# Seven products for w_out from tile 38 on, not 36; ten of batch 6's sixteen inverse blocks in one train with the last batch's, six ahead of it

## The chip, the cores and the metric

The kernel runs on one core of one Trainium2 chip. The metric is the device time of one execution in microseconds (us), the median of several runs.

## The reference

Two parts follow each other: a spectral layer (FFT along the sequence, a complex mix of 256 channels, soft shrinkage, inverse FFT) and a feed-forward part with a squared ReLU. All data are float32; 8 sequences (batches) of 3008 positions with 256 channels, 2048 hidden channels.

```
X = np.fft.rfft(x, axis=1)
Yr = Xr @ w_r - Xi @ w_i + b_r
Yi = Xr @ w_i + Xi @ w_r + b_i
Yr = np.sign(Yr) * np.maximum(np.abs(Yr) - lam, 0.0)
Yi = np.sign(Yi) * np.maximum(np.abs(Yi) - lam, 0.0)
y = np.fft.irfft(Y, n=x.shape[1], axis=1)
...
h = x @ w_in
r = np.maximum(h, 0.0)
g = r * r
return (g @ w_out).astype(np.float32)
```

## The kernel before

**Tiles and steps.** The feed-forward part runs over 48 tiles, six for each batch; a tile t holds about 500 positions, in two halves of 250 or 252. Batch 6 is tiles 36 to 41, batch 7 tiles 42 to 47. A tile is worked in 8 steps n, each on two of the 16 blocks of hidden channels. A step's first part (`first`, four products, 12 matmuls on TensorE) and second part (`second`, three products, 9 matmuls) multiply by w_in with seven products for a 2 by 2 block scheme; every product is three matmuls, since each number is split into a high and a low part. Their results are in four banks named psh; VectorE combines them (mp, mu, mv, mc), ScalarE squares and makes the high part mg, GpSimd the low part (`mg<-mc,mg`, two halves). Two steps later `out` multiplies by w_out into the two banks named pso: 6 matmuls for each of two halves, 12 of 500 columns in all. The main loop runs over m, half steps, so a step is two units of m and a tile 16. `then` fixes the order of these instructions on each engine.

**Seven products for w_out.** For tiles in `FREE`, in steps 1, 3 and 5 of the eight (`SEVEN`), `out_seven` takes seven products there as well: 21 matmuls of 250 columns instead of 12 of 500. It needs sums of the weights (`out_sums`, GpSimd), sums of g (`forms`), and two banks named psf that hold part of the results from step 1 to the end of the tile (`part`, `tile_sums`).

**The other work.** Between those steps stands the spectral layer of the later batches, as a list of jobs with a due time in units of m: forward blocks (`fwd_tasks`), pairs of frequency groups (`pair_tasks`: `fwd`, `mix`, `shrink`, `back`, lines 289, 310 and 343) and inverse blocks (`Back`, lines 553, 556 and 557). An inverse block gives 188 positions: for each of two channel halves three matmuls into one psf bank, a copy on ScalarE and an addition on VectorE (dy). All these share the two psf banks with the seven products. For each of the batches 6 and 7 all 16 blocks are computed ahead of their tiles: `load` or `load_two` (two blocks in one load, tiles th, tl, ts) fetches du from DRAM, `mm` computes, `keep` stores dy to DRAM (y), and `raw_load` fetches a whole tile's share back (yr) when its tile comes near. From yr the token sums are made: in `back_tasks` for ordinary tiles (`Tokens.sums`, `Tokens.split`, GpSimd and ScalarE), and by `Tokens.free` during the tile before where that tile is in `FREE`. `Tokens.free` keeps its sums in the tile ts, whose one buffer is also that of `load_two`.

**Where batches 6 and 7 stand.** `kept_tasks(B - 2, ...)` puts batch 6 into four groups of four blocks, a group every 16 units from 486.55 on, blocks 2.2 units apart; u, u2 and dy of such a block are all in the three buffers of xt. The pairs of batch 7 run from 489 to 547 at 5.25 units. `late` opens the tiles th, tl, ts and wsh, wsl, and the 16 blocks of batch 7 follow as a train from 554.85 on, 1.4 units apart. Tile 36 begins at 576.

**Order.** What `then` doesn't fix is placed by a scheduler that works with estimated times; the order on each engine is fixed before the program runs. DMAs that load are chained on SyncE's queue (`load_next`), which also issues the stores.

Of the kernel before, what the change touches and what calls it, by code (L numbers as in the profile page):

```python
# [24 lines left out]
B, S, D, FF = 8, 3008, 256, 2048  # L25
# [5 lines left out]
HALF = (252, 252, 250, 250, 250, 250)  # L31
HM = max(HALF)
NF = FF // 128
# [23 lines left out]
B11, B21, B22, T1, T3, T2, T4 = range(7)  # L57
ENDS = B - 2
TURN0, TURNS, PACE = 92, J, 6
FREE = range(ENDS * len(HALF), B * len(HALF) - 1)  # L60
SEVEN = (1, 3, 5)


# [1 line left out]
def fnet_moe(ctx: ExitStack, tc, x, w_r, w_i, b2, w_in, w_out, bm, cm, dx, am2, a32, c32, d32, out):  # L65
# [34 lines left out]
    def T(name, shape, dt, tag=None):  # L100
        tag = tag or name
        return pools.get(tag, phase["pool"]).tile(shape, dt, name=name, tag=tag, bufs=phase["bufs"].get(tag, 2))

    def bank(shape, name="psf"):
        return phase["psum"].tile(shape, F32, name=name, tag=name, bufs=phase["bufs"].get(name, 1))
# [281 lines left out]
    class Fwd32(Fwd):  # L387
# [8 lines left out]
        def mm(self):  # L396
            n = self.n
            self.ps = []
            for t in range(2):
                u = T("x2", [M1, 2, D], F32, tag="small")  # L400
                eng = pool if t and self.r == 1 else dve
                cut = eng.tensor_tensor(
                    out=u[:, :n], in0=self.xt[:M1, :n, 0], in1=self.xt[:M1, :n, 1], op=(ALU.add, ALU.subtract)[t]
                )
                if eng is pool:
                    self.far = cut
                else:
                    self.cut = cut
                ps = bank([128, 2, D])
                nc.tensor.matmul(ps[:M1, :n], am32[:, t], u[:, :n], start=True, stop=True)  # L410
                self.ps.append(ps)
# [85 lines left out]
    W2 = 4 * N2  # L497
    raw, yts, back_last = {}, {}, {}

    class Back:  # L500
# [40 lines left out]
        def mm(self):  # L541
            if self.b == 0:
                return self.mm32()
            if self.b == ENDS or self.b > ENDS and self.q % 5 % 2 == 0:
                y = T("dy", [128, 512], F32, tag="xt")[:, :2 * W2].rearrange("p (c w) -> p c w", c=2)
            else:
                y = T("dy", [128, 2, W2], F32)
            self.y = y
            for c in range(2):
                cs = slice(c * 128, c * 128 + 128)  # L550
                ps = bank([128, 2, 256])[:, :, :W2]
                pv = ps.rearrange("c j (p t) -> c j p t", p=2)
                mm = nc.tensor.matmul(pv[:, :, 0], self.u[:, 0, cs], dx_sb[:, 0], start=True, stop=False)  # L553

                with tc.issue_after(mm.ins):
                    nc.tensor.matmul(pv[:, :, 1], self.u[:, 1, cs], dx_sb[:, 0], start=False, stop=False)  # L556
                nc.tensor.matmul(ps[:, 0], self.u2[:, cs], dx_sb[:, 1], start=False, stop=True)  # L557
                self.done = copy(act, y[:, c], ps[:, 1])
                if self.b >= ENDS:
                    self.cut = dve.tensor_add(out=y[:, c], in0=ps[:, 0], in1=y[:, c])  # L560
                    continue
                for n, (t, lo, hi, at) in enumerate(self.spans):
                    if n == c == 0 and t not in raw:
                        raw[t] = T("yr", [128, 2, 2 * HM], F32)
                    o = y[:, c, lo:hi] if n else raw[t][:, c, at:at + hi - lo]
                    self.cut = dve.tensor_add(out=o, in0=ps[:, 0, lo:hi], in1=y[:, c, lo:hi])
# [141 lines left out]
    class Step:  # L708
        def __init__(self, t, n):
            self.t, self.n, self.h = t, n, tiles[t][2]  # L710
            self.end = t == len(tiles) - 1 and n == NF // 2 - 1
            self.seven = t in FREE and n in SEVEN

        def product(self, ps, a, b, terms=range(3)):
            yh, yl = yts[self.t]
# [69 lines left out]

        def out_seven(self, j):
            t, h, n = self.t, self.h, self.n
            i = SEVEN.index(n)
            if i == j == 0:
                part[t] = [bank([128, 512])[:, :2 * h].rearrange("p (j h) -> p j h", j=2) for _ in range(2)]  # L790
            low, high = [a[:, :2 * h].rearrange("p (j h) -> p j h", j=2) for a in acc[t]]
            p16, p57 = part[t]
            f = 2 * n
            plain = [[w[:, f + k, d * 128:(d + 1) * 128] for w in wout] for d, k in ((0, 0), (0, 1), (1, 1))]
            sums = [[w[:, i, k] for w in ws] for k in range(4)]
            g, tf = self.g, (self.th, self.tl)
            if j == 0:
                todo = ((p16[:, 0], plain[0], g, 0), (low[:, 0], plain[1], g, 2), (low[:, 1], sums[3], g, 3))
            else:
                todo = (  # L800
                    (p57[:, 0], sums[0], tf, 0), (p57[:, 1], sums[2], tf, 1),
                    (p16[:, 1], sums[1], tf, 2), (high[:, 0], plain[2], tf, 3),
                )
            for q, (x, y) in enumerate(((0, 0), (1, 0), (0, 1))):
                for at, (ps, a, b, k) in enumerate(todo):
                    then(
                        pe, pe.matmul, ps, a[x], b[y][:, k],
                        start=i == q == at == 0, stop=i == len(SEVEN) - 1 and q == 2 and j == 1 and at in (1, 2),
                    )

        def finish(self, pc, pd):
# [17 lines left out]
        def out(self, j):  # L829
# [14 lines left out]
            if f == NF - 1:  # L844
                b, c0, _ = tiles[t]
                if t in FREE:
                    o = last_sums.pop(t)
                else:
                    o = T("mo", [128, 4 * HM], F32, tag="ms")[:, :4 * h].rearrange("p (d h) -> p d h", d=2)
                for d in range(2):  # L850
                    if t in FREE:
                        then(dve, dve.tensor_add, out=o[:, d], in0=acc[t][d][:, :2 * h], in1=o[:, d])
# [35 lines left out]
    def back_tasks(t, start):  # L888
        b, c0, h = tiles[t]
        new = range(-(-c0 // W2), -(-(c0 + 2 * h) // W2))  # L890
        if b >= ENDS:
            new = ()
        jobs = []
        for j, q in enumerate(new):
            k, at = Back(b, q), start + 2.2 * j
            back_last[t] = k
            ahead = 1.6 if j == 0 and t > 1 and t % len(HALF) == 1 else 0.55 if j else 0.0
            jobs += [(at - ahead, k.load), (at + 1.6, (lambda k=k: behind(k.mm)) if t == 1 else k.mm)]
            if len(k.spans) > 1:
                jobs += [(start + 14.6, k.put)]  # L900
        if t > FREE[0]:
            return [(start, lambda: raw_load(t))]
        if t == FREE[0]:
            jobs += [(start, lambda: raw_load(t))]
        k = Tokens(t)
        if t == 0:
            return jobs + [(start + 7.1, k.begin)]
        for j in range(2):
            jobs += [(start + 7.1 + j, lambda j=j: k.sums(j))]
        for j in range(4):  # L910
            jobs += [(start + 9.1 + 1.2 * j, lambda j=j: k.split(j))]
        return jobs

    def raw_load(t):
        b, c0, h = tiles[t]
        raw[t] = T("yr", [128, 2, 2 * HM], F32)
        load_next(raw[t][:, :, :2 * h], ys[b][:, :, c0:c0 + 2 * h])

    def kept_tasks(b, start, step, wait):
        ks = [Back(b, q) for q in range(S // W2)]  # L920
        jobs = []
        for q, k in enumerate(ks):
            if b < B - 1:
                at = start + NF * (q // 4) + step * (q % 4)
                jobs += [(at, k.load)]
            else:
                at = start + step * q
                if q % 2 == 0:
                    jobs += [(at, lambda k=k, o=ks[q + 1]: k.load_two(o))]
            jobs += [(at + wait, k.mm), (at + wait + 1.0, k.keep)]  # L930
        return jobs

    def late():
# [82 lines left out]
    for r in range(-1, len(units) + 3):  # L1016
# [5 lines left out]
        k = r - 2  # L1022
# [12 lines left out]
        n, odd = divmod(k, 2)  # L1035
# [5 lines left out]
        if k >= 1 and odd and early:  # L1041
            q = early.pop(0)
# [35 lines left out]
    first = sorted(back_tasks(0, 0), key=lambda j: j[0])  # L1078
    kind = {"load": 0, "mm": 1}
    first = [[job for _, job in first if kind.get(job.__name__, 2) == k] for k in range(3)]  # L1080
# [25 lines left out]
    jobs = []  # L1106
# [7 lines left out]
    for b in range(2, B):  # L1114
        start = TURN0 + (b - 2) * TURNS * PACE
# [1 line left out]
        if b + 1 < B:  # L1117
            jobs += fwd_tasks(b + 1, start + 4)
    for t in range(1, len(tiles)):
        jobs += back_tasks(t, NF * (t - 1) + (-1.5 if t == FREE[0] else 0.5))  # L1120
    over = TURN0 + (B - 3) * TURNS * PACE
    jobs += kept_tasks(B - 2, NF * 30 + 6.55, 2.2, 2.15)
    done = over + PACE + 1.0 + 11 * 5.25 + 7.5
    jobs += [(done + 0.5, late)] + kept_tasks(B - 1, done + 0.6, 1.4, 2.4)
    jobs += [(done + 3.0 + 6.0 * j, lambda n=n: out_sums(n)) for j, n in enumerate(SEVEN)]
    jobs.sort(key=lambda j: j[0])
    for m in range(2 * len(steps) + 4):
        n, k = divmod(m, 2)
        if k and 0 <= n - 2 < len(steps):
            steps[n - 2].out(1)  # L1130
        if n < len(steps):
            t, i = divmod(n, NF // 2)
            ahead = k and t in FREE and i in (0, 2, 4, 6)
# [117 lines left out]
```

## Time and profile before

| | us |
|---|---|
| median of 3 runs (lowest to highest) | 2592.17 (2591.49 to 2594.46) |
| the profiled execution | 2589.44 |
| its span, first to last instruction | 2587.5 |
| TensorE matmul busy in the span | 2565.2 |
| VectorE / GpSimd / ScalarE busy | 1907.2 / 1761.2 / 1417.7 |

TensorE is called busy for 99% of the span, but a matmul's busy time runs on while the next has begun, so a busy TensorE may be working below its pace. The chain of work that ended last is TensorE for 97%. The granted clock is full but for two short stretches; the page's 40 slices show one of them.

### The profile page before, as it was taken

The numbers are of one execution on the slowest core, as the hardware profiler recorded it, in microseconds if no ns is written. First come the engines' busy times: TensorE is split into PE (matmuls) and PEld (weight loads), VectorE is DVE, ScalarE is ACT, GpSimd is POOL, SyncE is SP. The second block draws the span as 40 slices with busy tenths as digits, with TensorE's granted clock in tenths as the row PEclk, the third lists the DMA queues.
The fourth block names the chain that finished last, engine by engine and source line by source line (L and its number), as shares of the span: only waits on it lengthen the run. The fifth ranks groups of instructions, "written<-read, shape, count | busy, mean of one in ns | idle before, by whom it ended". The sixth has DMA issues, their size and how long they took to land.

```text
span 2587.5 us, 48058 instructions
## 1 busy us (share of the span) xinstructions
PE 2565.2 (99%) x17507; PEld 2373.7 (92%) x17507; DVE 1907.2 (74%) x3797; ACT 1417.7 (55%) x2175; POOL 1761.2 (68%) x1684
## 2 busy tenths in 40 slices
PE   9999999999999999999999999999999999999999
PEld 7899999999999999999999999999898989999998
DVE  7876766777777777777777777776676668888886
ACT  5655555555555555555555555555555545555554
POOL 1167666777676776677767676675555858888885
PEclk9999999999999999999999999999999989999999
DMA  9632332333333333433333333434334321000000
GB/s 312 197 94 86 113 101 76 108 110 106 102 107 113 103 109 102 119 106 102 104 111 113 109 99 106 118 97 119 118 112 124 119 85 33 23 27 25 25 25 17
DMA packets 192001, 257.03 MB, mean 99 GB/s; under 512 B 18376, under 2 KB 138176, under 8 KB 191768
## 3 DMA queue, kind: packets, MB, share of 16 engines
q1 hardware_dynamic: 178353, 228.71, 28.7%
q0 software_dynamic: 13280, 25.16, 4.1%
q8 instruction: 140, 2.29, 0.4%
q14 instruction: 93, 0.76, 0.1%
q10 hardware_dynamic: 135, 0.12, 0.0%
HBM read 150.36 MB, written 103.55 MB: 98 GB/s over the span
## 4 chain that ended last, share of the span: by engine, by line
PE 97%; DVE 2%; DMA 1%; ACT 0%; issue 0%; POOL 0%; SPq 0%; DVEq 0%; POOLq 0%; ACTq 0%
PE pso L592 38%; PE psh L592 36%; PE psf L310 7%; PE psf L289 3%; PE psf L343 2%; PE psf L251 2%; PE psf L592 2%; PE psf L475 1%; PE psf L557 1%; PE psf L556 1%; PE psf L553 1%; PE psf L373 1%; PE psf L530 1%; PE psf L410 0%; PE psf L485 0%; PE psf L461 0%
## 5 line engine op out<-in xcount | busy, mean ns | idle before, releaser
L113 POOL TENSOR_TENSOR mg<-mc,mg 128x500 fp32r<-128x500 f32 (+1 forms) x766 | 995.3, 1320 | 402.8 <-ACT mg L109 304.4
L592 PE MATMUL pso<-mg,wout 128*128 128x500 f32 (+2 forms) x4311 | 1086.1, 389 | 2.7 <-POOL mg L113 2.7
L592 PE MATMUL psh<-yt,win 128*128 128x250 f32 (+1 forms) x8064 | 1072.9, 280 | 0.8 <-DVE mc L592 0.3
L592 PEld LDWEIGHTS psh<-yt,win 128*128 128x128 f32 x8064 | 1019.0, 189 | 27.5 <-DVE yt L113 0.6
L592 PEld LDWEIGHTS pso<-mg,wout 128*128 128x128 f32 x4311 | 773.3, 189 | 125.7 <-POOL mg L113 3.0
L592 ACT ACTIVATE mc<-mc 128x1000 f32<-128x1000 f32 (+1 forms) x384 | 400.4, 1043 | 458.7 <-DVE mc L592 457.7
L592 DVE CUSTOM_DVE_ANT_0 mc<-psh,mv 128x250 f32<-128x250 f32 (+3 forms) x769 | 418.6, 546 | 286.3 <-PE psh L592 244.1
L109 ACT CAST mg<-mc 128x1000 fp32r<-128x1000 f32 (+1 forms) x385 | 396.8, 1031 | 14.5 <-POOL mg L113 0.4
L592 DVE TENSOR_TENSOR mv<-psh,mu 128x500 f32<-128x500 f32 (+1 forms) x384 | 260.9, 679 | 46.8 <-PE psh L592 12.4
L310 PE MATMUL psf<-wx,kxh 128*128 128x256 f32 x1008 | 211.4, 283 | 3.0 <-ACT kxh L109 1.3
L110 DVE COPY mp<-psh 128x250 f32<-128x250 f32 (+1 forms) x384 | 160.2, 417 | 53.1 <-PE psh L592 29.4
L331 DVE TENSOR_TENSOR kv<-psf,ke 64x256 f32<-64x256 f32 x336 | 141.8, 422 | 51.1 <-PE psf L310 35.6
L310 PEld LDWEIGHTS psf<-wx,kxh 128*128 128x128 f32 x1008 | 168.2, 190 | 6.1 <-ACT kxh L109 1.5
L592 DVE TENSOR_TENSOR mu<-psh,mp 128x250 f32<-128x250 f32 (+1 forms) x384 | 160.9, 419 | 12.4
L222 POOL TENSOR_TENSOR xs<-xt 120x256 f32<-120x256 f32 x156 | 120.0, 789 | 61.9 <-DMA xt<-x_in 21.7
L592 DVE CUSTOM_DVE_ANT_0 mc<-psh,mp 128x250 f32<-128x250 f32 (+1 forms) x384 | 156.8, 408 | 6.4 <-PE psh L592 6.3
L113 POOL TENSOR_TENSOR ksl<-kv,ksh 128x512 fp32r<-128x512 f32 x84 | 109.5, 1304 | 70.7 <-ACT ksh L109 66.4
L109 ACT COPY dy<-psf 128x188 f32<-128x188 f32 (+2 forms) x229 | 71.3, 314 | 152.7 <-PE psf L557 150.5
L310 PE MATMUL psf<-wx,kxl 128*128 128x256 f32 x504 | 142.2, 282 | 0.3 <-DVE kxl L113 0.3
L113 POOL TENSOR_TENSOR yt<-yr,yt 128x250 fp32r<-128x250 f32 (+1 forms) x94 | 88.3, 939 | 36.9 <-ACT yt L109 36.4
L333 ACT ACTIVATE kc<-kv,low 128x512 f32<-128x512 f32 x84 | 60.8, 724 | 84.5 <-DVE kv L331 84.3
L322 DVE TENSOR_TENSOR ke<-psf,bias 128x512 f32<-128x512 f32 x84 | 57.8, 688 | 59.2 <-PE psf L310 59.0
(164 smaller groups left out, 3180.5 us busy)
## 6 DMA issues: line engine op xcount, KB each, us to landing
ka<-s SPq DMA_DIRECT2D x96, 256.0 KB, 3.0
du<-s SPq DMA_DIRECT2D x96, 256.0 KB, 2.9
kcm<-cm_in POOLq DMA_DIRECT2D x84, 256.0 KB, 3.8
s<-kuh SPq DMA_DIRECT2D x84, 256.0 KB, 3.5
s<-kul SPq DMA_DIRECT2D x84, 256.0 KB, 3.7
s<-xe SPq DMA_DIRECT2D x82, 240.0 KB, 2.4
xt<-x_in SPq DMA_DIRECT2D x81, 240.0 KB, 3.2
out<-mo SPq DMA_DIRECT2D x64, 250.0 KB, 2.2
```

What stands on the lines that cost most here:

```text
L109: return act.copy(out=out, in_=in_)
L110: return eng.tensor_copy(out=out, in_=in_)
L113: return eng.tensor_tensor(out=out, in0=a, in1=b, op=ALU.subtract)
L222: return eng.tensor_tensor(out=out[:, :n], in0=self.xt[:, :n, 0], in1=self.xt[:, :n, 1], op=(ALU.add, ALU.subtract)[t])
L251: nc.tensor.matmul(ps[:, t], am_sb[0][:, j, t], v[:, t], start=n == 0, stop=n == 2)
L289: nc.tensor.matmul(pv[:, :, c, g, :], self.a[:, g, c * 128:(c + 1) * 128], bg, start=True, stop=True)
L310: self.last = nc.tensor.matmul(ps, l, wx[j][:, k, c, :], start=n == 0, stop=n == 5)
L322: dve.tensor_add(out=self.e, in0=self.pe, in1=bias)
L331: dve.tensor_add(out=v[64 * r:64 * r + 64, g], in0=ps[gs], in1=self.e[gs, r])
L333: act.activation(r, v, AF.Relu, bias=low)
L343: nc.tensor.matmul(ps[:, g], self.cm[:, g, j * 128:(j + 1) * 128], r[:, g], start=n == 0, stop=n == 2)
L592: last_of[eng] = op(*args, **kwargs)
```

## The change

- `FREE` begins at tile 38: tiles 36 and 37 take the ordinary 12 matmuls in all eight steps and get their token sums from `back_tasks`; so does tile 38, while 39 to 46 go on as before.
- `SPARE = 6`: of batch 6's 16 blocks the first six stand alone, from 488 on, 10.5 units apart, with 3.4 units from load to matmul (it was 2.15). Their dy is in xt.
- The other ten are put at the head of batch 7's train and loaded two at a time with `load_two`: 26 blocks from 554.85 on, 1.4 units apart, where there were 16. Their dy buffers alternate between dy and xt as batch 7's do.
- The loads of yr for tiles 36 to 38 come 2.5 units later than their jobs' start; that of 36 came 2 units before the usual start.
- In `Step` and `out_seven` the list of steps becomes a member (`sevens`); for the tiles that use it, it is the same list.

```diff
-FREE = range(ENDS * len(HALF), B * len(HALF) - 1)
+FREE = range(ENDS * len(HALF) + 2, B * len(HALF) - 1)
+SPARE = 6
...
-            if self.b == ENDS or self.b > ENDS and self.q % 5 % 2 == 0:
+            if self.b >= ENDS and (self.b == ENDS and self.q < SPARE or self.q % 5 % 2 == 0):
...
-        if t == FREE[0]:
-            jobs += [(start, lambda: raw_load(t))]
+        if b >= ENDS:
+            jobs += [(start + 2.5, lambda: raw_load(t))]
...
-    def kept_tasks(b, start, step, wait):
-        ks = [Back(b, q) for q in range(S // W2)]
+    def kept_tasks(ahead, start, step):
+        first, *ks = [[Back(b, q) for q in range(S // W2)] for b in range(ENDS, B)]
+        ks = first[SPARE:] + ks[0]
         jobs = []
+        for q, k in enumerate(first[:SPARE]):
+            at = ahead + 10.5 * q
+            jobs += [(at, k.load), (at + 3.4, k.mm), (at + 4.4, k.keep)]
         for q, k in enumerate(ks):
-            if b < B - 1:
-                at = start + NF * (q // 4) + step * (q % 4)
-                jobs += [(at, k.load)]
-            else:
-                at = start + step * q
-                if q % 2 == 0:
-                    jobs += [(at, lambda k=k, o=ks[q + 1]: k.load_two(o))]
-            jobs += [(at + wait, k.mm), (at + wait + 1.0, k.keep)]
+            at = start + step * q
+            if q % 2 == 0:
+                jobs += [(at, lambda k=k, o=ks[q + 1]: k.load_two(o))]
+            jobs += [(at + 2.4, k.mm), (at + 3.4, k.keep)]
...
-        jobs += back_tasks(t, NF * (t - 1) + (-1.5 if t == FREE[0] else 0.5))
+        jobs += back_tasks(t, NF * (t - 1) + 0.5)
     over = TURN0 + (B - 3) * TURNS * PACE
-    jobs += kept_tasks(B - 2, NF * 30 + 6.55, 2.2, 2.15)
     done = over + PACE + 1.0 + 11 * 5.25 + 7.5
-    jobs += [(done + 0.5, late)] + kept_tasks(B - 1, done + 0.6, 1.4, 2.4)
+    jobs += [(done + 0.5, late)] + kept_tasks(over + 6.0, done + 0.6, 1.4)
```

The order on the engines differs from m = 486 to about m = 614 and is the same elsewhere. Lines of the changed kernel are one higher from line 61 on, two from 714 on. Names: psf is one of the two shared banks, psh and pso those of the products with w_in and w_out, kb,ka a pair's first products, wx its mix, dx_sb,du an inverse block.

TensorE at m = 544, in tile 34 before the change: a pair's first products, two half blocks and the next mix, with no product of the tile between them.

```order
L289 MATMUL psf<-kb,ka 128x2x64 x4
L553 MATMUL psf<-dx_sb,du 128x2x94
L556 MATMUL psf<-dx_sb,du 128x2x94
L557 MATMUL psf<-dx_sb,du 128x188
L553 MATMUL psf<-dx_sb,du 128x2x94
L556 MATMUL psf<-dx_sb,du 128x2x94
L557 MATMUL psf<-dx_sb,du 128x188
L310 MATMUL psf<-wx_81,kxh 128x256
```

The same pair's first products in the changed kernel (m = 546):

```order
L593 MATMUL psh_25184<-yt_24900,win_84 128x250
L344 MATMUL psf<-ksl,kcm 128x256
L344 MATMUL psf<-ksh,kcm 128x256 x2
L344 MATMUL psf<-ksl,kcm 128x256
L593 MATMUL psh_25184<-yt_24901,win_83 128x250
L593 MATMUL psh_25268<-yt_24900,win_83 128x250
L593 MATMUL psh_25268<-yt_24900,win_84 128x250
L290 MATMUL psf<-kb,ka 128x2x64 x4
```

In the piece before, 15 groups on psf follow each other from m = 543.9 to 544.5 with three short runs of psh matmuls between them; in the changed order no more than five do anywhere from 486 on, and most stand alone between products of the tile.

TensorE at m = 581, where tile 36's first step is multiplied by w_out, before the change (nine half blocks in a row follow from the third row from the end on):

```order
L592 MATMUL pso_26854<-mg_26739,wout_86 128x504
L553 MATMUL psf<-dx_sb,du 128x2x94
L556 MATMUL psf<-dx_sb,du 128x2x94
L557 MATMUL psf<-dx_sb,du 128x188
L592 MATMUL pso_26855<-mg_26739,wout_85 128x504
L592 MATMUL pso_26855<-mg_26739,wout_86 128x504
L553 MATMUL psf<-dx_sb,du 128x2x94
L556 MATMUL psf<-dx_sb,du 128x2x94
L557 MATMUL psf<-dx_sb,du 128x188
```

The same place in the changed kernel:

```order
L593 MATMUL pso_26665<-mg_26543,wout_85 128x504
L554 MATMUL psf<-dx_sb,du 128x2x94
L557 MATMUL psf<-dx_sb,du 128x2x94
L558 MATMUL psf<-dx_sb,du 128x188
L593 MATMUL pso_26666<-mg_26543,wout_85 128x504
L593 MATMUL psh_26643<-yt_26233,win_83 128x252
```

The train's last half block stands at m = 601 now (it was 581), one at a time, and the first matmul of the seven products at m = 615 (it was 583). On GpSimd, the first use of the tile ts by `Tokens.free` at the start of tile 36, before the change:

```order
L113 TENSOR_TENSOR mg_26580<-mc,mg_26579 128x500 x2
L113 TENSOR_TENSOR mg_26652<-mc,mg_26651 128x500 x2
L113 TENSOR_TENSOR ts<-yr 128x252 x2
L113 TENSOR_TENSOR mg_26740<-mc,mg_26739 128x504 x2
L592 TENSOR_TENSOR ts<-yr,ts 128x252
```

And in the changed kernel, at the start of tile 38:

```order
L114 TENSOR_TENSOR mg_27511<-mc,mg_27510 128x504 x2
L114 TENSOR_TENSOR mg_27566<-mc,mg_27565 128x504 x2
L114 TENSOR_TENSOR ts<-yr 128x250 x2
L114 TENSOR_TENSOR mg_27626<-mc,mg_27625 128x500 x2
L593 TENSOR_TENSOR ts<-yr,ts 128x250
```

It moved from the end of the train to some 14 units behind it. SyncE's queue around the load of yr for tile 36, before:

```order
L120 DMA du<-s_7_75 128x1024
L120 DMA du<-s_7_75 64x2x256 x2
L120 DMA yr<-y_76 128x2x504
L858 DMA out<-mo 128x500 x2
L580 DMA y_77<-dy 256x1x188
```

and in the changed kernel:

```order
L581 DMA y_76<-dy 256x1x188
L121 DMA du<-s_6_74 128x1024
L121 DMA du<-s_6_74 64x2x256 x2
L581 DMA y_76<-dy 256x1x188
L121 DMA yr<-y_76 128x2x504
L581 DMA y_76<-dy 256x1x188
```

The load of yr stood behind the train's second pair of blocks, and stands behind the third now, and behind two stores.

## Rows read from the trace of the kernel before

**Rows 1.** Stretches: busy PE, PEld, DVE, ACT, POOL; clock, DMA share, GB/s.

```profile
1500.00:1800.00 300.00, 300.00 (x2075) 278.93 (x2074) 217.26 (x439) 167.33 (x262) 208.03 (x202) 1.00 0.37 106
1800.00:2115.00 315.00, 301.22 (x1999) 276.08 (x1999) 200.96 (x442) 158.21 (x264) 188.16 (x186) 0.96 0.39 118
```

**Rows 2.** Chain, full clock: start us, us, engine, line, matmuls.

```profile
1808.57 0.09 PE psf L553
1808.66 0.11 PE psf L556
1808.77 0.11 PE psf L557
...
1823.71 1.41 PE psf L310 x12
...
1849.03 0.71 PE psf L343 x6
...
1945.98 0.89 PE psf L289 x8
```

**Rows 3.** The chain: two steps' products with w_out, one after the other.

```profile
1949.09 2.74 PE pso L592 x12
...
1974.05 2.07 PE pso L592 x8
```

**Rows 4.** Matmuls, 1948.92 to 1974.05 us: count, busy, mean ns, idle, releasers.

```profile
L310 PE MATMUL psf<-wx,kxh 128*128 128x256 f32 x24 | 6.6, 346 | 1.7 <-DVE dy L566 0.6 <-DVE kul L113 0.6 <-DVE dy L560 0.5
...
L310 PE MATMUL psf<-wx,kxl 128*128 128x256 f32 x12 | 4.0, 333 | 0.0
...
L553 PE MATMUL psf<-dx_sb,du 128*128 128x188 f32 x7 | 2.6, 365 | 1.6 <-PE psf L289 0.6 <-DVE ke L322 0.4 <-DMA du<-s 0.3
...
L343 PE MATMUL psf<-ksh,kcm 128*128 128x256 f32 x8 | 2.0, 350 | 0.0
L343 PE MATMUL psf<-ksl,kcm 128*128 128x256 f32 x4 | 1.4, 350 | 0.0
```

**Rows 5.** The chain around tile 36's first product with w_out.

```profile
2079.79 2.49 PE pso L592 x11
...
2103.32 2.91 PE psh L592 x21
```

**Rows 6.** Matmuls by form, 2079.63 to 2103.11 us, as rows 4.

```profile
L592 PE MATMUL pso<-mg,wout 128*128 128x504 f32 x12 | 5.0, 561 | 2.7 <-POOL mg L113 2.7
L553 PE MATMUL psf<-dx_sb,du 128*128 128x188 f32 x12 | 4.4, 365 | 2.9 <-DVE dy L560 1.8 <-DMA du<-s 0.8
```

**Rows 7.** Waits, 1800 to 2115 us: in total, times, longest.

```profile
POOL ts L113 <- PE psf L557: 19.4, 1, 19.4
```

**Rows 8.** Shorter stretches, columns as rows 1.

```profile
1963.63:1974.05 10.42, 9.40 (x40) 8.49 (x41) 3.71 (x9) 2.39 (x6) 5.71 (x8) 0.53 0.63 164
...
2091.20:2103.11 11.91, 7.28 (x20) 5.65 (x21) 1.67 (x5) 1.94 (x7) 6.09 (x8) 0.50 0.38 121
...
1830.00:1850.00 20.00, 17.90 (x121) 16.14 (x120) 12.38 (x28) 9.79 (x19) 15.88 (x16) 1.00 0.27 81
1890.00:1902.30 12.30, 11.38 (x84) 10.60 (x83) 8.90 (x20) 7.29 (x12) 8.88 (x11) 1.00 0.23 65
```

**Rows 9.** The chain: start of one seven-product run, and what follows it.

```profile
2116.37 0.12 PE psf L592
...
2118.84 2.46 PE psh L592 x21
```

**Rows 10.** DMA issues, 2028 to 2110 us: count, KB, us to landing.

```profile
yr<-y SPq DMA_DIRECT2D x2, 504.0 KB, 5.7
```

**Rows 11.** Timeline in tile 35: loads, GpSimd's low parts, their products.

```profile
2042.11 1.83 SPq L120 DMA_DIRECT2D du<-s  x3
...
2045.64 2.49 POOL L113 TENSOR_TENSOR mg<-mc,mg 128x500 fp32r<-128x500 f32 x2
...
2049.09 1.08 PE L592 MATMUL pso<-mg,wout 128*128 128x500 f32 x4
```

More of the change, by code (lines that the diff above doesn't have):

```diff
@@ L711, in __init__ @@
             self.end = t == len(tiles) - 1 and n == NF // 2 - 1
-            self.seven = t in FREE and n in SEVEN
+            self.sevens = SEVEN if t in FREE else ()
+            self.seven = n in self.sevens
         def product(self, ps, a, b, terms=range(3)):
@@ L787, in out_seven @@
             t, h, n = self.t, self.h, self.n
-            i = SEVEN.index(n)
-            if i == j == 0:
+            i, begins = SEVEN.index(n), n == self.sevens[0]
+            if begins and j == 0:
                 part[t] = [bank([128, 512])[:, :2 * h].rearrange("p (j h) -> p j h", j=2) for _ in range(2)]
@@ L807, in out_seven @@
                         pe, pe.matmul, ps, a[x], b[y][:, k],
-                        start=i == q == at == 0, stop=i == len(SEVEN) - 1 and q == 2 and j == 1 and at in (1, 2),
+                        start=begins and q == at == 0, stop=i == len(SEVEN) - 1 and q == 2 and j == 1 and at in (1, 2),
                     )
```

## The prediction

> **What bounds the kernel now.** I read the totals first, then busy time by stretches, then the chain and the waits inside the stretches that fall behind. TensorE holds nearly the whole chain and is busy for nearly the whole span, so it is the bound throughout, and the question is only where it works below its pace. In a clean stretch, 1500 to 1800 us, it is busy for all of 300 us at full clock; from 1800 to 2115 us it is busy for 301.22 of 315 us at a mean clock of 0.96 [rows 1]. That is the whole stretch where the inverse blocks of batches 6 and 7 are computed ahead. Idle time (13.8 us) and lost clock (4% of 315 us, some 12 us) both lie there; after it nothing is lost.
>
> The 13.8 us of idle time understate the loss, because a matmul's busy time runs on after the next could have begun. So I count work instead, at prices from the chain at full clock: a step's 21 products with w_in 2.46 us [rows 9], its 12 with w_out 2.74 us [rows 3], a half block (lines 553, 556, 557) 0.09 + 0.11 + 0.11 = 0.31 us, twelve matmuls of line 310 1.41 us, six of line 343 0.71 us, a pair's first products 0.89 us [rows 2].
>
> *Stall A, tile 34.* One step's products with w_out begin at 1949.09 us, the next step's at 1974.05 us: 24.96 us [rows 3]. The work between: 2.74 + 2.46, 36 matmuls of line 310 (4.23), 12 of line 343 (1.42), seven half blocks (2.17) [rows 4], one pair's first products (0.89): 13.91 us. Lost: **11.05 us**. The matmuls waited for kp, dy, ke, kul and du in turn [rows 4]: 15 groups share two psf banks there with almost no products of the tile between them, so each waits until VectorE and ScalarE have emptied the bank of the one two before it. In the second half the clock is 0.53 [rows 8].
>
> *Stall B, tile 36's start.* From 2079.79 us to the next full run of w_in at 2103.32 us is 23.53 us [rows 5]; the work is two sets of 12 (5.48), one of 21 (2.46) and twelve half blocks (3.72) [rows 6]: 11.66. Lost 11.87 us, and the run at 2103.32 took 2.91 for 2.46 us [rows 5], still at low clock: **12.3 us** in all. Two things meet here. The last half blocks of the train stand in a row before the seven products, which need both psf banks; and GpSimd stood for 19.4 us before its first operation on ts [rows 7], released by the last block's matmuls, since ts is also a buffer of the train's loads. The low parts (mg) are queued behind that operation, so TensorE waited for GpSimd as well [rows 6]. The clock was 0.50 [rows 8].
>
> *Small stalls C.* 2.10 us idle between 1830 and 1850 us and 0.92 us between 1890 and 1902.3 us [rows 8], each a pair and two blocks too close: **3.0 us**.
>
> A + B + C = 26.4 us.
>
> **A rule weighed.** Matmul busy time hides the loss here, as the work count shows. The Trainium skill (page "Trainium Kernel Development and Optimization", Best Practices) says to judge the distance to the limit not by matmul busy time but by the busy share of weight loads. By that: 278.93 of 300 us in the clean stretch is a share of 0.930; 276.08 us at that share are 296.9 us of work in 315, a loss of 18.1 us [rows 1], and the time would be 2592.2 - 18.1 + 1.6 = 2575.7 us, an estimate. I take the work count, since at half clock a weight load is busy longer as well and the share then passes for work.
>
> **The change, part by part.**
>
> 1. *Seven products two tiles later.* A run of 21 matmuls takes 2118.84 - 2116.37 = 2.47 us [rows 9], the 12 that take its place 2.74 [rows 3]: 0.27 us, times three steps, times two tiles: **+1.6 us**, all on TensorE and so on the path. ScalarE, VectorE and GpSimd lose the work of `forms`, which costs nothing and gives nothing, as they aren't the bound.
> 2. *The seven products' start.* The train's last half block stands 14 units of m, seven steps or some 40 us, ahead of the first seven products, and about 8 units ahead of the first use of ts. Neither the row of half blocks nor GpSimd's 19.4 us has a reason left. B goes: **-12.3 us**. The train itself cost nothing while it ran at this pace in tiles 35 and 36: up to 2079 us its half blocks stand between products. The same pace goes on for ten blocks more, and each is worth 0.62 us of TensorE that has only moved.
> 3. *Six blocks alone.* At 10.5 units a block comes about every five steps, its loads 3.4 units ahead of its matmuls, and each xt buffer is free long before the next needs it; the longest row of psf groups from 486 on is five, of pairs only. A goes (**-11.05 us**), and C (**-3.0 us**), where blocks met pairs. What remains in that stretch is like 1500 to 1800 us, where forward blocks, pairs and inverse blocks of a running batch stood together without idle time [rows 1].
> 4. *Queues.* The ten blocks take 15 loads in place of 30, each twice as large, and as many stores. SyncE's queue is in order, and the load of yr for tile 36 stands behind the third pair's loads, which wait for the first pair's matmuls. In the trace those loads were issued at 2042.11 us and took 1.83 us [rows 11]; with a store, yr is issued at some 2044.6 us and lands 5.7 us later at the median [rows 10]: 2050.3 us. GpSimd comes to it behind the low part of step 2, at 2045.64 + 2.49 = 2048.1 us [rows 11]: a wait of about 2 us, up to 3 us if GpSimd is earlier. The step's low part is first read by the fifth of its products, 2049.09 + 4 x 0.23 = 2050.0 us, and was ready after half of its 2.49 us, at 2046.9 us [rows 11]: a slack of 3.1 us. So I cost it at nothing; without that slack it would be 2 to 3 us. For tiles 37 and 38 the same count gives a wait near zero: yr is issued about when the block two pairs earlier is done, some 1.5 units before GpSimd needs it.
>
> Sum: -11.05 - 12.3 - 3.0 + 1.6 = -24.75 us. The profiled execution took 2589.44 us, so the changed one would take 2564.7 us profiled; it lay 2.7 us under the median of the runs. Against the median: 2592.17 - 24.75 = **2567.4**, say 2567.5 us. The best case is that nothing at all is lost from 1800 to 2115 us; for small gaps of some tenths that A, B and C leave out I allow 3 us, so 2564, and 2563 with the runs' own spread.
>
> **Rivals.**
>
> *One stall comes back in another form.* Ten blocks more in a train that must keep up with du's loads, a late yr at tile 36, 37 or 38, or pairs that crowd without blocks. For it: the order was made with estimated times, and A and B are both places where they were wrong. Against it: nothing in the new order has more than five psf groups in a row. Its size is about that of A: half of it waits, half the clock (10.42 us at 0.53 [rows 8] cost 4.9 us). 2592.2 - 12.3 - 3.0 + 1.6 = 2578.5 us if a stall of A's size is left; with one of B's size in its place, 2592.2 - 11.05 - 3.0 + 1.6 = 2579.8 us. After each long wait the clock was at half [rows 8], so a new wait pays twice. The Trainium skill says why (page "TensorE: Matmul & The Clock Gate", "What's actually happening": the throttled state is the default and activity releases it); the trace agrees, with 0.53 and 0.50.
>
> *Slower: yr late at three tiles.* Tiles 36 to 38 take their token sums from yr in SyncE's queue, behind loads that wait for the train. If each held GpSimd as long as ts did in B (19.4 us), each would cost 11.9 us: 2592.2 - 26.4 + 1.6 + 35.6 = 2603 us. It decides from 8.3 us of TensorE's time a tile on, that is waits of GpSimd over 8.3 + 3.1 = 11.4 us. Against it: a load of yr lands in 5.7 us [rows 10], and only being issued 10 us late would do it.
>
> *No change.* If the crowding came from batch 7's pairs and not from batch 6's blocks, and the wait at the seven products' start moved to tile 38 with them, A and B stay and only 1.6 us come: 2593.8 us. Against it: B's release was a block's matmul [rows 7].
>
> **How the numbers follow.** The forecast, 2563 to 2571 us, gets 0.73; the returning stall, up to 2580 us, 0.18; no change 0.05; slower 0.04. The range 2563 to 2580 us takes in the first two. A measurement tells 0.2%, 5.2 us, from no change: faster 0.91, same 0.05, slower 0.04.
>
> **What would show it.** In the changed profile TensorE should be busy for nearly all of the stretch that was 1800 to 2115 us and is some 25 us shorter, at clock 1.00; the wait of GpSimd's ts for a block's matmul should be gone; the steps of tiles 36 and 37 should have 12 matmuls of w_out at 2.74 us throughout. Wrong would be: a clock of about 0.5 anywhere from 1800 us on, GpSimd or ScalarE waiting for yr for over 3 us with TensorE idle behind it, or TensorE waiting for du within the longer train.

## The result and the profile after

| | before | changed |
|---|---|---|
| median, us (lowest to highest) | 2593.32 (2591.49 to 2594.95) | 2565.2 (2564.88 to 2570.2) |
| profiled execution, us | 2589.44 | 2564.88 |
| its span, us | 2587.5 | 2563.1 |
| TensorE matmul busy, us | 2565.2 | 2553.7 |

The ratio of the changed kernel to the one before is 0.9896, with a 95% interval from 0.9879 to 0.9913. The profiled executions differ by 24.56 us, their spans by 24.4, where -24.75 was forecast. The medians differ by 28.1 us, since the profiled execution of before lay 3.9 us below the median of its runs and that of the changed kernel 0.3 us. On a second chip the changed kernel had a median of 2566.06 us and a span of 2563.0 us against 2589.81 us before, a ratio of 0.9909 (0.9892 to 0.9925).

The stretches of the changed kernel, with the columns of [rows 1]. The second ends at 2089 us, since what ended at 2115 us now ends some 25 us earlier:

```profile
1500.00:1800.00 300.00, 300.00 (x2075) 278.96 (x2074) 218.16 (x436) 166.58 (x259) 209.00 (x203) 1.00 0.35 103
1800.00:2089.00 289.00, 288.20 (x1976) 266.97 (x1976) 195.44 (x431) 154.64 (x249) 187.57 (x184) 1.00 0.38 116
```

Idle time in the second stretch fell from 13.8 to 0.8 us, and the clock is 1.00 where it was 0.96. The place of stall A [rows 3], from the chain of the changed kernel (start us, us, what):

```profile
1944.62 2.77 PE pso L593 x12
1947.38 0.80 PE psh L593 x7
...
1948.55 1.30 PE psf L311 x11
...
1952.43 2.76 PE pso L593 x12
```

From one step's products with w_out to the next it is 7.81 us, and the pieces between stand near their prices. It was 24.96 us, with more work between (13.91 us at the prediction's prices). The place of stall B [rows 5], in the same view:

```profile
2095.86 2.28 PE pso L593 x10
2098.34 0.11 PE psf L558
2098.45 0.49 PE pso L593 x2
2098.93 1.27 PE psh L593 x11
...
2100.41 0.11 PE psf L558
```

The half blocks stand one by one between products of the tile, and none waits.

One new wait has come, and it is the one of part 4. The timeline of the changed kernel in tile 35 (start us, us, engine, line, operation; in brackets the idle time ahead and what ended it):

```profile
2027.50 1.43 POOL L114 TENSOR_TENSOR ms<-yr 128x252 f32<-128x252 f32 x2 [2.25 <-DMA yr<-y]
2028.89 1.96 POOL L114 TENSOR_TENSOR yt<-yr,yt 128x252 fp32r<-128x252 f32 x2
2030.80 1.29 POOL L114 TENSOR_TENSOR wsl<-st,wsh 128x512 fp32r<-128x512 f32 x1
2032.06 0.73 POOL L638 TENSOR_TENSOR ms<-yr,ms 128x252 f32<-128x252 f32 x1
...
2032.74 1.27 POOL L114 TENSOR_TENSOR yt<-ms,yt 128x504 fp32r<-128x504 f32 x1
...
2033.97 2.48 POOL L114 TENSOR_TENSOR mg<-mc,mg 128x500 fp32r<-128x500 f32 x2
...
2035.29 1.62 PE L593 MATMUL pso<-mg,wout 128*128 128x500 f32 x6 [0.80 <-POOL mg L114]
```

GpSimd waits 2.25 us for yr of tile 36, and behind four more groups of its operations the low part mg comes late enough that TensorE stands for 0.80 us.

### The profile page after: what moved, and what is told of

Its sections match the earlier page's. It is cut to its first block, busy times and chain, and to the rows that moved or that the text cites. A ratio compares the mean times of both kernels' runs of the same rounds, so it can differ in the third digit from the quotient of the medians.

```text
span 2563.1 us, 47855 instructions
## 1 busy us (share of the span) xinstructions
PE 2553.7 (100%) x17453; PEld 2363.8 (92%) x17453; DVE 1889.7 (74%) x3767; ACT 1412.9 (55%) x2167; POOL 1746.1 (68%) x1672
## 4 chain that ended last, share of the span: by engine, by line
PE 97%; DVE 1%; DMA 1%; POOL 0%; ACT 0%; issue 0%; SPq 0%; DVEq 0%; ACTq 0%
PE pso L593 39%; PE psh L593 36%; PE psf L311 7%; PE psf L290 3%; PE psf L344 2%; PE psf L252 2%; PE psf L593 1%; PE psf L476 1%; PE psf L557 1%; PE psf L558 1%; PE psf L554 1%; PE psf L374 1%; PE psf L531 1%; PE psf L411 0%; PE psf L486 0%; PE psf L462 0%
## 5 line engine op out<-in xcount | busy, mean ns | idle before, releaser
L593 PE MATMUL pso<-mg,wout 128*128 128x500 f32 (+1 forms) x4365 | 1099.1, 389 | 0.8 <-POOL mg L114 0.8
L110 ACT CAST mg<-mc 128x1000 fp32r<-128x1000 f32 (+1 forms) x385 | 396.8, 1031 | 13.8
L593 DVE TENSOR_TENSOR mv<-psh,mu 128x500 f32<-128x500 f32 (+1 forms) x384 | 260.9, 679 | 47.0 <-PE psh L593 12.3
L593 DVE TENSOR_TENSOR mu<-psh,mp 128x250 f32<-128x250 f32 (+1 forms) x384 | 160.9, 419 | 12.3
L114 DVE TENSOR_TENSOR xl<-xs,xh 120x512 fp32r<-120x512 f32 x78 | 93.2, 1195 | 7.8 <-ACT xh L110 7.8
```

The lines of the kernel that those rows point to most:

```text
L110: return act.copy(out=out, in_=in_)
L114: return eng.tensor_tensor(out=out, in0=a, in1=b, op=ALU.subtract)
L593: last_of[eng] = op(*args, **kwargs)
```

## The experiments

A table serves all of them ("changed" is the changed kernel, e1 to e11 are the experiments). It gives the time that TensorE lost in four places: for each matmul, the time to the next one's start less the median of that time for its line and shape in the same profile, summed over stretches of 10 us, of which those under 0.4 us are left out. C is 1820 to 1910 us, A 1930 to 1980, "mid" 1980 to 2060, B from there to 2140. Saved is the median of before less that of the kernel, both on the same chip; the interval is that of the ratio. Each count is of one profile; where an edit left C and A as they were (e1, e4, e8) the counts differ from those of before by up to 1.3 us, so smaller differences tell nothing.

| kernel | C | A | mid | B | saved, us | ratio (interval) |
|---|---|---|---|---|---|---|
| before | 4.2 | 11.3 | 0 | 12.4 | | |
| changed | 0 | 0 | 1.2 | 0 | 28.1; 23.8 on the second chip | 0.9896 (0.9879 to 0.9913) |
| e1 | 4.3 | 10.8 | 0 | 0 | 10.6 | 0.9965 (0.9952 to 0.9978) |
| e2 | 0 | 0 | 0 | 13.5 | 20.2, of which 6.2 are work left out | 0.9923 (0.9908 to 0.9937) |
| e3 | 0 | 0 | 1.2 | 7.0 | 18.9 | 0.9928 (0.9913 to 0.9943) |
| e4 | 5.5 | 11.9 | 0 | 10.3 | 1.5 | 0.9993 (0.9983 to 1.0002) |
| e5 | 0 | 0 | 1.2 | 0 | 21.0 | 0.9916 (0.9902 to 0.9931) |
| e6 | 0 | 0 | 0 | 0 | 26.4 | 0.9896 (0.9881 to 0.9911) |
| e7 | 1.1 | 8.0 | 1.1 | 12.5 | 4.0 | 0.9985 (0.9976 to 0.9995) |
| e8 | 4.2 | 11.4 | 0 | 8.1 | 4.2 | 0.9983 (0.9974 to 0.9992) |
| e9 | 0 | 0 | 0 | 7.8 | 20.4 | 0.9918 (0.9904 to 0.9933) |
| e10 | 5.3 | 8.9 | 0 | 0 | 12.1 | 0.9958 (0.9944 to 0.9972) |
| e11 | 6.9 | 10.1 | 6.3 | 0 | 4.9 | 0.9982 (0.9973 to 0.9992) |

### Each half of the change alone

**e1**: the seven products begin at tile 38, with the change's times for the loads of yr; all blocks stay as they were.

```diff
-FREE = range(ENDS * len(HALF), B * len(HALF) - 1)
+FREE = range(ENDS * len(HALF) + 2, B * len(HALF) - 1)
```

> The kernel before with one part of the change: the seven products (and the token sums of Tokens.free) begin at tile 38; all 32 blocks stand where they stood. Theory: stall B (12.3 us) goes since the train ends well before the seven products and the first use of ts, the two tiles cost 1.6 us, stalls A and C stay: 2593.3 - 12.3 + 1.6 = 2582.6 us, with the low clock in tile 34 still there and none at tile 36. Rival, the crowd of blocks itself is what costs and not what follows it: 2593.3 + 1.6 = 2594.9 us, with a stall wherever the train ends.

Measured 2579.38 us, 10.6 us less than before. B is gone whole and A and C stay, so B and the price of the six steps make the forecast -12.3 + 1.6 = -10.7 us. The interval reaches from 5.7 to 12.4 us less, so the agreement to 0.1 us is partly luck; that B goes and A and C stay is not.

**e2**: the seven products stay at tile 36; six blocks of batch 6 stand alone as in the change, and the other ten are left out: their half blocks aren't computed, and results of batch 7 are stored in their place.

```diff
+                if q >= SPARE:
+                    continue
-                at = start + NF * (q // 4) + step * (q % 4)
+                at = start + step * q
...
-    jobs += kept_tasks(B - 2, NF * 30 + 6.55, 2.2, 2.15)
+    jobs += kept_tasks(B - 2, over + 6.0, 10.5, 3.4)
```

> The kernel before with the seven products from tile 36 on and the train of batch 7 alone; of batch 6 only the first six blocks are computed, 10.5 units apart, and batch 7's blocks 6 to 15 are stored in the place of the other ten too. Left out are so 20 half blocks, 20 x 0.31 = 6.2 us of TensorE, and ten stores are added. Theory: A and C (14.05 us) go and B stays: 2593.3 - 14.05 - 6.2 = 2573.0 us; GpSimd's wait for the last block at ts is again near 19 us and the clock falls once, at tile 36. Rival, the three stalls feed each other and B shrinks with A: 2561 us.

Measured 2569.77 us (ratio 0.9923, 0.9908 to 0.9937), 20.2 us less, of which 20 half blocks of 0.31 us are 6.2: **14.0 us** for A and C, where 14.05 was forecast (the interval of the ratio is some 7 us wide). B stood, at 13.5 us by the count for 12.4 in before, and some 20 us earlier in time. The waits of e2 from 2050 to 2100 us (engine, line, what it waited for: us, times, longest):

```profile
POOL ts L114 <- DMA y<-dy: 20.1, 1, 20.1
...
PE psf L554 <- DVE dy L561: 3.9, 3, 2.5
```

GpSimd's wait at ts is there again, though the profile names a store as its end where it named a block's matmul in before. So the halves are worth about what each was said to be worth, and they add up: -10.6 - 14.0 = -24.6 us.

### What made B

The prediction named two things that meet in B: GpSimd held at ts, and the row of half blocks ahead of the seven products. These four runs take them apart.

**e4**: before, with the train's second loads in a tile of their own (tv), so that ts is free.

```diff
-            u2 = T("du", [128, 4, D], F32R, tag=("tl", "ts")[self.q // 2 % 2])[:, :2]
+            odd = self.q // 2 % 2
+            u2 = T("du", [128, 2, D] if odd else [128, 4, D], F32R, tag="tv" if odd else "tl")[:, :2]
```

> The kernel before, with the train's second loads in a tile of their own, so that Tokens.free's tile ts no longer waits for the train; the row of ten half blocks before the seven products stays, and the load of yr for tile 37 stays behind the train in SyncE's queue. Theory, ts and the row of half blocks share B: 4 to 6 us less, 2587 to 2589 us. Rival, the load of yr, issued behind the train's loads and landed 2 us before GpSimd began, would have held GpSimd nearly as long: 2 us less at most, 2591 to 2593 us, and GpSimd waits for yr instead.

Measured 2588.51 us, 1.5 us less, and the interval takes in no change: the rival's forecast, not the 4 to 6 us of the theory. From the timeline of e4:

```profile
2090.76 0.57 SPq L120 DMA_DIRECT2D yr<-y  x1
...
2096.60 1.39 POOL L113 TENSOR_TENSOR ts<-yr 128x252 f32<-128x252 f32 x2 [17.87 <-issue]
```

GpSimd stood for 17.87 us all the same. The profile names nothing that ended the wait ("issue"), but the times fit yr of tile 37: its load stands in SyncE's queue behind the train's own loads, was issued at 2090.76 us and landed 5.7 us later, at 2096.5. In before it was issued at 2089.58 us and landed 5.2 us later, at 2094.8, and ts came free at 2096.9 us. One wait had ended 2 us ahead of the other.

**e8**: e4, with that load of yr 5 units earlier as well.

```diff
-            return [(start, lambda: raw_load(t))]
+            return [(start - (5.0 if t == FREE[0] + 1 else 0.0), lambda: raw_load(t))]
```

> The kernel before with Tokens.free's ts no longer shared with the train (as e4) and the load of yr for tile 37 queued 5 units earlier; the seven products still begin at tile 36. Theory from e4, it was the late yr that held GpSimd and the order's row of half blocks came of it: B goes but for a rest, 9 to 12 us less than the kernel before, without the 1.6 us. Rival, the train's end beside the seven products costs by itself: 4 us less at most, with TensorE waiting at the last half blocks.

Measured 2585.92 us, 4.2 us less, about the rival's 4 us at most and not the 9 to 12 of the theory. GpSimd no longer waits at ts, but 8.1 us of B stay. TensorE's first matmuls of the last half blocks, from the timeline of e8:

```profile
2091.84 0.29 PE L553 MATMUL psf<-dx_sb,du 128*128 128x188 f32 x1
2093.61 0.35 PE L553 MATMUL psf<-dx_sb,du 128*128 128x188 f32 x1 [1.25 <-DVE dy L560]
2094.03 0.27 PE L553 MATMUL psf<-dx_sb,du 128*128 128x188 f32 x1
2095.90 0.35 PE L553 MATMUL psf<-dx_sb,du 128*128 128x188 f32 x1 [1.38 <-DVE dy L560]
2097.35 0.35 PE L553 MATMUL psf<-dx_sb,du 128*128 128x188 f32 x1 [0.87 <-DVE dy L560]
```

Two half blocks, 0.62 us of work, take some 2 us in the row: the next pair waits until ScalarE has copied and VectorE has added the pair before. By the count 5.5 of the 8.1 us are lost in the row. The rest, some 2.4 us, is lost by the seven products right behind it. After the first they wait for nothing, but they run at half clock: one begins every 0.21 us, where 2.47 / 21 = 0.12 us is the price [rows 9]. The stretch of e8 (columns as [rows 1]):

```profile
2100.00:2104.00 4.00, 4.00 (x21) 4.00 (x20) 0.00 (x0) 0.00 (x0) 1.82 (x2) 0.50 0.36 76
```

So with GpSimd out of the way the row and the low clock behind it hold B for 8.1 us, and 12.4 - 8.1 = 4.3 us came on top. Not all of these need be GpSimd's two waits: in before nine half blocks stand in the row and TensorE waits 1.5 us there for the train's own loads of du, in e8 the row has seven and no such wait.

**e3**: the changed kernel with the seven products from tile 37 on.

```diff
-FREE = range(ENDS * len(HALF) + 2, B * len(HALF) - 1)
+FREE = range(ENDS * len(HALF) + 1, B * len(HALF) - 1)
```

> The changed kernel with the seven products from tile 37 on (one tile earlier, the next is as before the change's first). The train still ends at about m = 597, the first use of ts is at 593 and the first seven products at 599; six half blocks stand in a row there. Theory: one tile gives 0.8 us, and GpSimd waits at ts for the train's end, some 8 us or more of wait, of which its slack covers 3: 2565.2 - 0.8 + 5 to 12 = 2569 to 2576 us, with a drop of the clock at tile 37. Rival, only the crowd at tile 36 mattered: 2564.4 us.

Measured 2571.06 us, as forecast. The longer train's end meets the seven products again, and 7.0 us are lost there. The waits of e3, 2090 to 2140 us:

```profile
POOL ts L114 <- PE psf L558: 13.3, 1, 13.3
...
PE pso L593 <- POOL mg L114: 2.6, 1, 2.6
```

**e9**: e3 with the tile tv, and the loads of yr for tiles 36 to 38 earlier, so that GpSimd should find at ts what it needs.

```diff
-            return [(start, lambda: raw_load(t))]
+            return [(start - (5.0 if t == FREE[0] + 1 else 0.0), lambda: raw_load(t))]
...
-            jobs += [(start + 2.5, lambda: raw_load(t))]
+            jobs += [(start + -1.5, lambda: raw_load(t))]
```

> The changed kernel with three things together: the train's second loads in a tile of their own (so ts isn't shared), the loads of yr for tiles 36 to 38 earlier, and the seven products from tile 37 on. In its order no row of half blocks stands before the seven products. Theory, what held e3 back was the queue and ts and not the crowd: 0.8 us for the tile and 1 us for yr, 1.8 us less than the changed kernel. Rival, the train's end still collides with tile 37: as e3, some 5 us more than the changed kernel.

Measured 2569.44 us, 3.4 us more than the changed kernel on the same chip where 1.8 less was the theory; 7.8 us of B are left, about as many as in e3. The wait of GpSimd at ts in e9, from the waits of 2080 to 2140 us:

```profile
POOL ts L114 <- issue: 7.7, 1, 7.7
```

The matmuls by form of e9, 2112 to 2126 us (columns as [rows 4]):

```profile
L554 PE MATMUL psf<-dx_sb,du 128*128 128x188 f32 x8 | 2.3, 293 | 2.0 <-DVE dy L561 2.0
...
L594 PE MATMUL psf<-mg,wout 128*128 128x252 f32 x2 | 1.0, 499 | 0.9 <-DVE dy L561 0.9
```

GpSimd still waits 7.7 us at ts: the load of yr that it needs was issued at 2106.59 us, behind a load of the train, and landed 5.3 us later. TensorE loses only 1.0 us by that (0.74 us of idle, waiting for mg). And a row stands before the seven products after all: five half blocks from 2119.66 us on with no product of the tile between them. Half blocks and then the seven products wait for VectorE's dy, and the seven products run at half clock from 2125 us on. So what sets B in e8 and e9 is for the most part the row of half blocks, which has to be through the two psf banks before the seven products can have them, and the half clock behind it. The distance of two tiles takes away both causes, which neither a tile of its own nor these earlier loads do.

### What made A

**e7**: before, with the sixteen blocks evenly spaced instead of in four groups.

```diff
-                at = start + NF * (q // 4) + step * (q % 4)
+                at = start + step * q
...
-    jobs += kept_tasks(B - 2, NF * 30 + 6.55, 2.2, 2.15)
+    jobs += kept_tasks(B - 2, NF * 30 + 6.55, 4.1, 2.15)
```

> The kernel before with all 16 blocks of batch 6 where they were, but evenly 4.1 units apart and not in groups of four; lead, buffers and tile 36 as before. In its order 16 groups on psf still stand in a row at m = 544. Theory of the prediction, blocks too close to each other make A and C: 11 to 14 us less than the kernel before. Rival, the number of blocks between the pairs counts, since they delay tile 34's own inverse blocks and so its tokens: A stays, within 4 us of the kernel before.

Measured 2586.12 us, 4.0 us less: the rival's forecast. C falls from 4.2 to 1.1 us, but A keeps 8.0 of 11.3. So "too close" explains most of C and the smaller part of A.

**e10**: e1, with the last group of four moved to the head of the train; twelve blocks stay where they were.

```diff
-SPARE = 6
+SPARE = 12
...
-            at = ahead + 10.5 * q
-            jobs += [(at, k.load), (at + 3.4, k.mm), (at + 4.4, k.keep)]
+            at = ahead + NF * (q // 4) + 2.2 * (q % 4)
+            jobs += [(at, k.load), (at + 2.15, k.mm), (at + 3.15, k.keep)]
```

> Seven products from tile 38 on; the first twelve of batch 6's blocks stay in their three groups of four, and only the last group (blocks 12 to 15) moves to the head of the train. It is to tell what makes stall A at tile 34 (10.8 us left when only the seven products moved, 2579.4 us). Theory: A is the last group alone, whose loads and matmuls stand right behind tile 34's own three blocks and ahead of its token sums, on the one buffer du's chain of loads and the two psf banks. Then A goes and C stays: 2579.4 - 10.8 = 2568.6 us, 2567 to 2571, and VectorE's additions that write yr for tile 34 end before 1950 us. Rival: the lag builds up over all sixteen blocks and the pairs of batch 7, and a row of pair groups waits on the two psf banks at m = 544 without those blocks as well: at least half of A stays, 2573 to 2579 us.

Measured 2577.64 us, 12.1 us less than before, 1.5 more than e1 saved. A keeps 8.9 us: the rival's forecast. The chain of e10 through A:

```profile
1953.48 0.09 PE psf L554
...
1953.68 0.12 PE psf L558
...
1953.82 0.34 SPq L121
...
1954.69 2.95 DMA du<-s
...
1957.78 0.34 PE psf L558
...
1958.49 0.23 DVE yr L567
...
1958.81 0.62 POOL ms L114
```

The first rows are a half block of tile 34's own second inverse block. When it is done, SyncE can issue the load of its third, since the running batch has a single du buffer; the load's last DMA is on the chain for 2.95 us, and only then come the last half blocks, yr, and the token sums of tile 34 on GpSimd. The chain of before goes the same way at 1952.76 to 1957.95 us, and there is nothing about it in the prediction. In the changed kernel the last yr for tile 34 is written at 1938.77 us; in before it is 1958.78, in e10 1959.63.

**e11**: e1, with tile 34's own blocks and token sums 3 units earlier.

```diff
-        jobs += back_tasks(t, NF * (t - 1) + 0.5)
+        jobs += back_tasks(t, NF * (t - 1) + (-2.5 if t == ENDS * len(HALF) - 2 else 0.5))
```

> Seven products from tile 38 on, all sixteen blocks of batch 6 in their four groups as before; only tile 34's own three inverse blocks and its token sums come 3 units of m (some 8 us) earlier. Theory: TensorE stands in A because tile 34's token sums come late, behind its own blocks, which wait in the queue of loads among batch 6's. Then moving these jobs by 8 us takes most of A away: 2579.4 - 8 = 2571.4 us, 2569 to 2574. Rival: the row of groups on the two psf banks sets A whatever tile 34's tokens do: within 2 us of 2579.4 us.

Measured 2584.91 us, 4.9 us less and outside both forecasts: A keeps 10.1 us, and 6.3 us are lost anew at 2020 to 2040 us. The edit did only half of what it was for: the third block's load was issued at 1949.08 us in place of 1953.10, but its yr was still written at 1958.19 us. The chain of e11 through A:

```profile
1960.54 0.98 PE psf L311 x6
...
1962.03 0.42 DVE kv L332
...
1964.12 2.30 DVE kv L335
...
1968.49 0.34 DVE kp L301
```

The load of tile 34's third block is off the chain, and VectorE's work on the pairs, which has to empty the psf banks, holds TensorE nearly as long. So A seems to have two holds as well: the own blocks' late load, and the row of pairs on two banks. Six blocks that stand 10.5 units apart, with their loads 3.4 units ahead, take both away, as e2 and the changed kernel show; even spacing of all sixteen (e7) and moving the last group alone (e10) don't. Which of the number, the distance and the lead of the blocks does it isn't shown, since all three changed together, and how A divides between the two holds isn't settled either.

### The price of the seven products, and yr

**e5**: the changed kernel with the seven products from tile 44 on, 18 more steps with 12 matmuls.

```diff
-FREE = range(ENDS * len(HALF) + 2, B * len(HALF) - 1)
+FREE = range(ENDS * len(HALF) + 8, B * len(HALF) - 1)
```

> The changed kernel with the seven products for w_out from tile 44 on only: six tiles more take the ordinary twelve. Theory: 0.27 us x 3 steps x 6 tiles = 4.9 us more than the changed kernel in the same job, all on TensorE. Rival: VectorE and GpSimd, fuller in tiles with seven products, hold them back, so that the price is near zero.

Measured 2568.79 us (ratio 0.9916, 0.9902 to 0.9931): 2.7 us over the changed kernel on the same chip by the medians, 2567.0 - 2563.0 = 4.0 us by the spans. A step that goes without the seven products costs 4.0 / 18 = 0.22 us (0.15 by the medians), where 0.27 was priced from the rows; the theory's 4.9 us in all was too much.

**e6**: the changed kernel with the loads of yr for tiles 36 to 38 4 units earlier.

```diff
-            jobs += [(start + 2.5, lambda: raw_load(t))]
+            jobs += [(start - 1.5, lambda: raw_load(t))]
```

> The changed kernel with the loads of yr for tiles 36 to 38 queued 4 units earlier; tile 36's stands behind the train's second pair again. Theory: the wait of GpSimd for yr at tile 36 (2.2 us in the changed kernel, 0.8 us of it reaching TensorE) goes, and with it the loss of 1.2 us there: 1 us less than the changed kernel in the same job. Rival: the wait is covered by slack, no difference.

Measured 2563.41 us (2563.17 to 2563.72; ratio to before 0.9896, 0.9881 to 0.9911), with a span of 2561.8 us, 1.2 us under that of the changed kernel on the same chip. In this timeline GpSimd's low part after the load is early again:

```profile
2025.24 2.50 POOL L114 TENSOR_TENSOR mg<-mc,mg 128x500 fp32r<-128x500 f32 x2
...
2028.74 1.99 PE L593 MATMUL pso<-mg,wout 128*128 128x500 f32 x8
```

No wait of TensorE for GpSimd is left between 1800 and 2300 us. It is the fastest of all the kernels here, though its interval overlaps that of the changed kernel.

## Why the prediction was right, and where its steps were not

- **The sum** was -24.75 us; the profiled executions differ by 24.56. It came from counting work, not idle time. TensorE's idle time in the stretch was 13.8 us, and the loss counted over all matmuls is 4.2 + 11.3 + 12.4 = 27.9 us. The prediction's 26.4 us left small gaps out (C was 3.0 for 4.2). That the sum still came within 0.2 us is luck in part: the loss was 1.5 us larger than counted, but 1.2 us of new loss came with the late yr, and the medians say 28.1 and 23.8 us on two chips.
- **The rule weighed** would have given 18.1 us of loss and 2575.7 us. The measurement decides for the work count: 2565.2 us. The Trainium skill (page "Trainium Kernel Development and Optimization", Best Practices) is right not to judge by matmul busy time, but the busy share of weight loads, read against the clean stretch, missed a third of the loss here. The prediction's reason accounts for a good part of that: a weight load took 5.65 / 21 = 0.27 us where the clock was 0.50 [rows 8] and 278.93 / 2074 = 0.13 us in the clean stretch [rows 1], so slow loads passed for work.
- **Part 1** (+1.6 us): e5's step price makes it 6 x 0.22 = 1.3 us (0.9 by the medians). Right in sign, a little over.
- **Part 2** (-12.3 us): e1 confirms the size within its interval. Of its two reasons the row of half blocks weighs most (8.1 us by e8, with the half clock behind it). GpSimd's 19.4 us [rows 7], the most striking row of all, was worth 2.1 us of B by itself (e4, whose time can't be told from no change) and at most 4.3 with the wait that stood beside it. That the longer train would run at no cost held: no stretch of 10 us between 2060 and 2140 us loses 0.4 us.
- **Part 3** (-14.05 us): e2 confirms the size within its interval; by the count C and A are 15.5 us, and B grew by 1.1 us in e2, so the match to 0.05 us is luck. The reason was half right. "Too close" holds for C; in A the chain ran first through SyncE's load of tile 34's own third block and then through the pairs. The prediction named only the second, because it counted the matmuls' releasers [rows 4] and didn't follow the chain between the two rows of [rows 3].
- **Part 4** (nothing): the wait for yr came as worked out, 2.25 us for "about 2". What failed is the slack of 3.1 us [rows 11]: it was read off the low part that GpSimd makes ahead of the wait. The wait shifts the next one, in front of which stand four more groups of GpSimd's operations, and that one had less slack than the 2.25 us. So 0.8 us of idle, 1.2 us by the count, reached TensorE where nothing was set down, and e6 gets 1.2 us of span back.
- **The rivals.** "One stall comes back" didn't happen, but e3 and e9 show what it would have cost one tile earlier: 7.0 and 7.8 us, less than the 11 to 12 it was priced at. "yr late at three tiles" needed waits of GpSimd over 11.4 us; its longest for yr was 2.25. "No change" fell with e1 and e2: each half does its part.
- **"A new wait pays twice"** holds only in part. In e1 stall A ran at a higher clock than in before, as the stretches from 1963 to 1974 us show, first before and then e1:

```profile
1963.00:1974.00 11.00, 9.48 (x42) 8.45 (x41) 4.23 (x11) 3.02 (x8) 6.34 (x8) 0.56 0.60 155
```

```profile
1963.00:1974.00 11.00, 8.99 (x50) 7.91 (x51) 5.12 (x12) 3.85 (x10) 6.47 (x8) 0.84 0.55 143
```

The mean clock is 0.84 for 0.56, and A's whole loss 10.8 us for 11.3. Matmuls that waited for their banks anyway lost little by running slower, so the 4.9 us set down for half clock aren't a price on top of the wait in A. Where the work behind a wait filled TensorE it did pay: the seven products of e8 lost some 2.4 us at a clock of 0.50.

## What to carry to other kernels

Count a stall as elapsed time less work at clean prices, then look for a second hold behind the first: in stall B two waits of GpSimd ended some 2 us apart, with a row of matmul groups beside them. Taking the first away gave 1.5 us of 12, and moving the work to where none of them arises gave it all. Size a stall's causes by taking them away one at a time, not by the longest wait in it: GpSimd's 19.4 us were worth some 2 us. Count the slack of a new wait on an in-order engine over everything queued behind it.

## What the runs showed of the hardware

How long the clock stays low isn't fixed by the stall: the same stall A, with a loss of 10.8 and 11.3 us, had a mean clock of 0.84 in e1 and 0.56 in before over the same 11 us (one profile of each). And small groups that share two banks went at a pace set by ScalarE and VectorE, which had tile 36's own work between the copies and additions: two half blocks of 0.31 us each took some 2 us in the row (e8), about three times their work, at full clock until 2096 us.
